# Another order for the first 18 head pairs of cosine attention fused with a hard-swish MLP

## The chip, the cores and the metric

One core of a Trainium2 chip runs the whole program. The metric is the device time of one execution in microseconds (us): the median over several executions. The kernel before takes 426.46 us (median of 4 runs, 425.51 to 426.71).

## The reference

```python
q_n = q / (norm(q, axis=-1) + 1e-6)              # q, k, v: (8, 12, 448, 64)
k_n = k / (norm(k, axis=-1) + 1e-6)
attn = softmax(q_n @ k_n.T / tau)                # tau = 0.1
x = (attn @ v).transpose(0, 2, 1, 3).reshape(3584, 768)
h = x @ w_in                                     # (768, 2048)
g = h * clip(h + 3, 0, 6) / 6
out = g @ w_out                                  # (2048, 768)
```

Since the rows of q_n and k_n have length 1, the scores are bounded, and the kernel leaves the maximum out of the softmax.

## The kernel before, in words

The 8 x 12 heads are worked as 48 pairs (heads n and n + 6 of one batch), six pairs to a batch. Loads go by two pairs: load j brings q or k of pairs 2d and 2d + 1, d = j // 2, and one load of v serves the same two pairs.

For each load there is a chain: LQ (the load, a DMA on SyncE's queue, SP), SQ (squares), RE (sum of each row on VectorE, DVE), NO (four small ACT operations that give one over the norm, for q and k together), NM (multiplication, result in bf16), then a transposition. Loads 0 to 13 are transposed on TensorE (PE) by TR and copied out of PSUM by CQ, CK and CS; loads from 14 on are transposed by a DMA, XD, after which CK (on DVE) and CS (on POOL) only make the padded keys, and scores read the transposed queries in place. VC brings v to bf16. SC multiplies keys by queries, EX takes the exponential on ScalarE (ACT) from PSUM, VA multiplies the result by v and a column of ones into PSUM, FI divides by the sum (a reciprocal and a product on DVE). The attention output of a pair goes transposed into `xT`: by a DMA (XB), or by PE (BK) with a copy (CX).

A batch's six pairs make one `xT`, on which the MLP runs in units. A first-layer unit (kind 1 in ORDER, lines 490 to 521) is 6 matmuls of 448 columns, a relu on ACT (UA) and a product on DVE (UV) into `gT`; a second-layer unit (kind 2, lines 523 to 557) is 16 matmuls of 384 columns, a copy out of PSUM, and two stores on SP. U issues the next unit. W issues the next of eight weight loads on GpSimd's (POOL's) queue, where they are cast to bf16; the first two hold the first half of w_in's columns, the next two the second half, the last four w_out. Units 0 to 7 of a batch need the first two, units 8 to 15 the second two, second-layer units all of w_out.

Nothing schedules this at build time: each engine runs its instructions in the order in which they are written out, and waits where data or a buffer isn't there. For pairs 0 to 17 the order is PLAN, a text of operations; `SQ.5.a.0.7` is the square of load 5 on ACT, columns 0 to 6, and the letter v, p or a names the engine (DVE, POOL, ACT). From pair 18 on a loop (line 682) issues the rest by a fixed pattern. Buffers that tie operations together: 7 for raw loads (LQ j waits for NM j - 7), 3 for raw v, 4 for bf16 v, 2 for squares, 3 for normalised loads, 2 for padded keys, 3 for transposed loads.

PSUM: until OPEN the scores of pairs 0 to 5 alternate between two pairs of banks (SC), while banks Y and Z take transposes. OPEN, after the last exp of pair 5, closes these, and scores, units and transposes then take turns in a ring of six banks (M0, M1, Y, Z, M2, M3): the seventh user waits until the first is read. DP.n and D.n issue n matmuls on zeros whose results are not used, of 248 columns (line 603) and 512 columns (line 598).

Of the kernel before, what the change touches and what calls it, by code (L numbers as in the profile page):

```python
# [15 lines left out]


FIRST = 18
ORDER = "111111111111111111111111111112212222"

PLAN = [
    "DP.4 LQ.1 DP.2 SQ.1.a.11.3 SQ.1.a.0.4 LQ.0 DP.2 LQ.3 SQ.1.a.4.3 DP.5 LQ.2 SQ.0.a.8.6 SQ.0.p.6.2 DP.4",
    "SQ.1.v.7.4 SQ.0.p.0.6 DP.3 RE.1.1 RE.1.0 RE.0.1 DP.1 NO.0.1 LQ.5 DP.4 RE.0.0 SQ.3.a.0.7 DP.2 NO.0.0 NM.1.v.0",
    "NM.0.p.1 DP.8 NM.1.v.1 SQ.2.a.0.7 RE.3 LQ.4 SQ.5.a.0.7 TR.1.Y DP.11 RE.2 NM.0.p.0 SQ.4.p.0.7 CK.0.v TR.0.Z",
    "NO.1 DP.2 CQ.0.v SC.0.0.0 RE.5 DP.3 DP.2 EX.0.0 SC.0.1.1 EX.0.1 DP.3 SC.0.2.0 LV.0 LQ.8 CK.1.v RE.4 LQ.7",
    "EX.0.2 CQ.1.v VC.0.p NM.2.p LQ.6 DP.6 SC.0.3.1 VA.0.0 NM.3.p LV.1 VC.1.v VA.0.1 SC.1.0.0 EX.0.3 VA.0.2 TR.2.Z",
    "VA.0.3 DP.3 SC.1.1.1 LV.2 NO.2 EX.1.0 FI.0 TR.3.Y SC.1.2.0 LQ.9 EX.1.1 NM.4.p CK.2.v VA.1.0 EX.1.2 CQ.2.v",
    "VA.1.1 VC.2.v SC.1.3.1 CQ.3.v NM.5.p SQ.7.p.0.7 SC.2.0.0 DP.2 EX.1.3 VA.1.2 EX.2.0 SC.2.1.1 EX.2.1 CK.3.v",
    "VA.1.3 SC.2.2.0 TR.4.Y BK.0.Z FI.1 SC.2.3.1 DP.2 EX.2.2 DP.1 EX.2.3 CQ.4.v SQ.6.p.0.7 W CX.0.v SC.3.0.0",
    "EX.3.0 CQ.5.v RE.7 TR.5.Z VC.3.v SC.3.1.1 VA.2.0 W VA.2.1 EX.3.1 VA.2.2 VA.2.3 RE.6 CK.4.v SQ.9.a.0.7",  # L30
    "SC.3.2.0 EX.3.2 SC.3.3.1 D.10 LQ.10 LQ.11 SC.4.0.0 CK.5.v FI.2 VA.3.0 NO.3 RE.9 SQ.8.p.0.7 NM.7.p EX.3.3",
    "BK.2.Z RE.8 EX.4.0 SC.4.1.1 VA.3.1 EX.4.1 SC.4.2.0 VA.3.2 EX.4.2 BK.1.Y CX.2.v VA.3.3 SC.4.3.1 LV.3 SC.5.0.0",
    "VC.4.v NM.6.p DP.2 EX.4.3 SC.5.1.1 EX.5.0 TR.7.Z CX.1.v TR.6.Y LV.4 EX.5.1 FI.3 SC.5.2.0 VC.7.p VA.4.0 EX.5.2",
    "VC.6.v CK.6.v NO.4 SC.5.3.1 VA.4.1 EX.5.3 VA.4.2 VC.5.p CS.6.v VA.4.3 DP.5 CQ.6.v CQ.7.v SQ.11.p.0.7 OPEN",
    "SQ.10.p.0.7 CS.7.v CK.7.v FI.4 RE.11 SC.6.0 SC.6.1 EX.6.0 EX.6.1 BK.3 SC.6.2 VA.5.0 NM.8.p VA.5.1 EX.6.2",
    "CX.3.v VA.5.2 VA.5.3 FI.5 SC.6.3 SC.7.0 SC.7.1 TR.8 XB.4 EX.6.3 VA.6.0 LQ.13 VA.6.1 EX.7.0 RE.10 NM.9.p",
    "SC.7.2 EX.7.1 CQ.9.v VA.6.2 EX.7.2 BK.5 TR.9 CQ.8.v LQ.14 CX.5.v SC.7.3 VA.6.3 VC.9.p CK.9.v U NO.5 FI.6 U U",
    "UA UA VA.7.0 EX.7.3 VA.7.1 UA CS.9.v UV W CS.8.v CK.8.v SC.8.0 UV UV SC.8.1 NM.10.p VA.7.2 VA.7.3 FI.7 EX.8.0",
    "SC.8.2 LQ.12 VC.8.p W EX.8.1 TR.10 U LV.5 EX.8.2 UA VA.8.0 CQ.11.v SC.8.3 SQ.13.p.0.7 VA.8.1 CQ.10.v UV",
    "SC.9.0 SC.9.1 EX.8.3 NM.11.p EX.9.0 RE.13 VA.8.2 SC.9.2 VA.8.3 FI.8 EX.9.1 SC.9.3 LQ.15 EX.9.2 U UA TR.11",  # L40
    "SQ.12.p.0.7 EX.9.3 RE.12 CS.11.v VA.9.0 VA.9.1 VC.10.p U CK.10.v XB.6 NO.6 NM.12.p VC.11.p SQ.15.p.0.7",
    "CK.11.v SC.10.0 CS.10.v UV VA.9.2 U UA SC.10.1 EX.10.0 UV UA EX.10.1 SC.10.2 VA.9.3 EX.10.2 LV.6 U UV UA",
    "TR.12 LQ.17 LQ.16 CQ.12.v XB.7 SC.10.3 U SQ.14.p.0.7 NM.13.p UV CQ.13.v SC.11.0 UA RE.15 FI.9 EX.10.3 EX.11.0",
    "U U UV UA UA VA.10.0 SC.11.1 EX.11.1 UV SC.11.2 EX.11.2 VA.10.1 UV VA.10.2 TR.13 SC.11.3 LQ.19 U LV.7 CS.12.a",
    "UA VA.10.3 RE.14 NO.7 SQ.17.p.0.7 NM.15.p CS.13.v CK.13.a U U FI.10 EX.11.3 UA VA.11.0 VA.11.1 VA.11.2",
    "NM.14.p SQ.16.a.0.7 UA CK.12.v SC.12.0 RE.17 XB.8 UV W U VA.11.3 VC.12.p U UV UV EX.12.0 FI.11 SC.12.1 UA",
    "XB.9 UV VC.15.p UA UV EX.12.1 LQ.18 SC.12.2 XB.10 VA.12.0 BK.11 SC.12.3 SC.13.0 EX.12.2 CX.11.v VA.12.1 XD.15",
    "U EX.12.3 EX.13.0 SC.13.1 SC.13.2 UA W U EX.13.1 VA.12.2 RE.16 SQ.19.p.0.7 VC.13.a VA.12.3 EX.13.2 UV SC.13.3",
    "UA U XD.14 FI.12 NO.8 UV SQ.18.p.0.7 CK.14.v U U EX.13.3 U VA.13.0 UA UV SC.14.0 UA UA UA EX.14.0 UV CS.14.v",
    "VC.14.a UV UV SC.14.1 EX.14.1 U SC.14.2 UA NM.16.v RE.19 UV EX.14.2 VA.13.1 U UA U W VA.13.2 UA RE.18 UV UV",  # L50
    "CK.15.v U LQ.20 SC.14.3 UA NO.9 XD.16 UV LQ.21 VA.13.3 U FI.13 U U NM.17.p XD.17 XB.13 UA VA.14.0 UV VA.14.1",
    "SC.15.0 UA EX.14.3 XB.12 VA.14.2 LV.8 UV UA UV EX.15.0 VA.14.3 SC.15.1 W EX.15.1 SC.15.2 FI.14 SQ.21.a.0.7",
    "CK.16.v EX.15.2 SC.15.3 SQ.20.a.0.2 U EX.15.3 U VA.15.0 SQ.20.p.2.5 VA.15.1 NM.19.v RE.20 UV SC.16.0 VC.17.v",
    "CS.16.v SC.16.1 UA CK.17.v SC.16.2 XD.19 EX.16.0 VC.16.v VA.15.2 RE.21 LQ.22 VA.15.3 U EX.16.1 EX.16.2",
    "SC.16.3 FI.15 UA NM.18.p U UV U XD.18 EX.16.3 UA NO.10 VA.16.0 VA.16.1 SC.17.0 SQ.22.p.0.7 SC.17.1 LV.9",
    "VC.18.p UV CK.18.v RE.22 EX.17.0 SC.17.2 VA.16.2 NM.20.v LV.11 XB.14 EX.17.1 VA.16.3 U LQ.23 VC.19.a SC.17.3",
    "UA U EX.17.2 FI.16 XB.16 UV CK.19.v LV.10 CS.18.v EX.17.3 VA.17.0 XB.15",
]


# [1 line left out]
def kernel(  # L62
# [608 lines left out]
    by_kind = {"1": [u for u in stream if u[0] is mm1_unit], "2": [u for u in stream if u[0] is mm2_unit]}  # L671
    first = [by_kind[x].pop(0) for x in ORDER]
    stream = first + [u for u in stream if u not in first]
# [91 lines left out]
```

## Time and profile before

| | |
|---|---|
| median of the runs | 426.46 us |
| the profiled execution | 427.59 us |
| its span, first to last instruction | 425.8 us |
| PE busy | 413.4 us (97%) |
| ACT busy | 271.3 us (64%) |
| DVE busy | 218.3 us (51%) |
| POOL busy | 181.4 us (43%) |
| moved by DMA | 65.82 MB |
| granted TensorE clock, mean | 0.998 |

The numbers below come from one execution taken by the hardware profiler. Matmuls overlap in the records, so the busy time of PE is not its time at full rate: the distance from one matmul's start to the next tells more. A wait in the profile names the instruction or transfer that came last before the waiting instruction could start. The chain of work that ended last is followed back from the last instruction to whatever released each one. SPq and POOLq are instructions that issue DMAs; the time to landing runs from the issue to the completion of the transfer.

### The profile page before, as it was taken

The numbers are of one execution on the slowest core, as the hardware profiler recorded it, in microseconds if no ns is written. First come the engines' busy times: TensorE is split into PE (matmuls) and PEld (weight loads), VectorE is DVE, ScalarE is ACT, GpSimd is POOL, SyncE is SP. The second block draws the span as 40 slices with busy tenths as digits, with TensorE's granted clock in tenths as the row PEclk, the third lists the DMA queues.
The fourth block names the chain that finished last, engine by engine and source line by source line (L and its number), as shares of the span: only waits on it lengthen the run. The fifth ranks groups of instructions, "written<-read, shape, count | busy, mean of one in ns | idle before, by whom it ended". The sixth has DMA issues, their size and how long they took to land.

```text
span 425.8 us, 9251 instructions
## 1 busy us (share of the span) xinstructions
PE 413.4 (97%) x3574; PEld 244.1 (57%) x3575; DVE 218.3 (51%) x419; ACT 271.3 (64%) x593; POOL 181.4 (43%) x184
## 2 busy tenths in 40 slices
PE   7999999899997999999999999999999999999996
PEld 5656655455654555655555555655555555665564
DVE  7689867485425454554555554455554344215410
ACT  6999989787355775676765685576675675105400
POOL 5997787322234474374373473473471310000000
PEclk9999999999999999999999999999999999999999
DMA  8997999997878669767879667567667251330033
GB/s 295 312 232 214 231 180 214 149 205 172 202 186 195 182 157 164 168 167 166 159 190 154 158 155 172 152 168 185 153 156 108 54 81 34 65 78 20 2 75 75
DMA packets 94156, 65.82 MB, mean 155 GB/s; under 512 B 58656, under 2 KB 92576, under 8 KB 94112
## 3 DMA queue, kind: packets, MB, share of 16 engines
q1 hardware_dynamic: 90320, 58.89, 60.6%
q0 software_dynamic: 3712, 6.29, 9.7%
q8 instruction: 28, 0.46, 0.5%
q14 instruction: 16, 0.13, 0.1%
q10 hardware_dynamic: 80, 0.05, 0.0%
HBM read 47.19 MB, written 11.01 MB: 137 GB/s over the span
## 4 chain that ended last, share of the span: by engine, by line
PE 77%; DMA 12%; ACT 4%; DVE 3%; SPq 2%; issue 1%; POOL 1%; ACTq 0%; POOLq 0%; DVEq 0%
PE M L532 21%; PE M L496 18%; PE PV L433 9%; DMA vr<-in_v_dram 5%; PE Y L496 5%; PE Z L532 5%; PE Y L532 5%; PE M L394 5%; PE Z L496 4%; DMA tT<-nrm 3%; ACT at L412 3%; DMA raw<-in_q_dram 2%; PE Z L394 1%; PE SC L394 1%; DVE n L215 1%; DMA xT<-on 1%
## 5 line engine op out<-in xcount | busy, mean ns | idle before, releaser
L532 PEld LDWEIGHTS <-gT 128*128 128x128 bf16 x912 | 88.7, 98 | 58.6
L412 ACT ACTIVATE at<-M 128x448 bf16<-128x448 f32 x195 | 94.8, 565 | 30.1 <-PE M L394 25.3
L496 PEld LDWEIGHTS <-w_in_sb 128*128 128x128 bf16 x768 | 74.2, 98 | 68.7 <-issue 5.0
L532 PE MATMUL M<-w_out_sb,gT 128*128 128x384 bf16 (+1 forms) x640 | 106.0, 322 | 0.0
L496 PE MATMUL M<-xT,w_in_sb 128*128 128x448 bf16 x510 | 104.2, 352 | 0.2 <-DVE gT L511 0.2
L246 POOL TENSOR_TENSOR nrm<-raw,r 128x896 bf16<-128x896 f32 (+1 forms) x45 | 74.3, 1657 | 26.0 <-ACT r L234 22.2
L203 POOL TENSOR_TENSOR sq<-raw 128x896 f32<-128x896 f32 (+3 forms) x42 | 67.8, 1620 | 26.4 <-DMA raw<-in_k_dram 11.4
L511 DVE SCALAR_TENSOR_TENSOR gT<-u,M 128x448 bf16<-128x448 bf16 x85 | 52.4, 620 | 49.8 <-ACT u L505 48.7
L505 ACT ACTIVATE u<-M,half_bias 128x448 bf16<-128x448 f32 x85 | 55.0, 651 | 21.3 <-PE M L496 19.8
L433 PEld LDWEIGHTS <-at 128*128 128x128 bf16 x1344 | 53.3, 98 | 25.5 <-issue 18.3
L433 PE MATMUL PV<-vx,at 128*128 128x65 bf16 (+1 forms) x1344 | 63.9, 198 | 0.0
L215 DVE TENSOR_REDUCE n<-sq 128x14 f32<-128x896 f32 (+1 forms) x50 | 51.9, 1041 | 3.6 <-ACT sq L201 2.4
L351 POOL COPY km<-tT 64x128 bf16<-64x128 bf16 x34 | 10.7, 314 | 99.2 <-DMA tT<-nrm 46.0
L543 ACT COPY o<-M 128x384 f32<-128x384 f32 (+1 forms) x21 | 9.9, 472 | 41.4 <-PE M L532 37.4
L394 PE MATMUL M<-tT,kz 64*128 64x448 bf16 (+1 forms) x172 | 34.3, 353 | 1.5 <-DVE gT L511 0.6
L449 DVE TENSOR_TENSOR on<-PV,rc 128x512 bf16<-128x512 f32 x48 | 33.2, 692 | 3.7 <-DMA xT<-on 2.1
L545 DVE COPY o<-M 128x384 f32<-128x384 f32 (+1 forms) x19 | 10.4, 547 | 47.3 <-PE M L532 44.6
L412 ACT ACTIVATE at<-Y 128x448 bf16<-128x448 f32 x48 | 27.3, 569 | 10.0 <-PE Z L394 10.0
L412 ACT ACTIVATE at<-Z 128x448 bf16<-128x448 f32 x51 | 28.8, 565 | 3.0 <-PE M L394 2.7
L496 PE MATMUL Y<-xT,w_in_sb 128*128 128x448 bf16 x138 | 29.9, 352 | 0.7 <-DMA w_in_sb<-in_moe_w_in_dram 0.7
L448 DVE RECIPROCAL rc<-PV 128x8 f32<-128x8 f32 x48 | 9.9, 206 | 37.7 <-PE PV L433 34.4
L496 PE MATMUL Z<-xT,w_in_sb 128*128 128x448 bf16 x120 | 26.1, 353 | 2.2 <-DMA xT<-on 2.2
(78 smaller groups left out, 345.8 us busy)
## 6 DMA issues: line engine op xcount, KB each, us to landing
vr<-in_v_dram SPq DMA_DIRECT2D x96, 128.0 KB, 3.8
raw<-in_k_dram SPq DMA_DIRECT2D x24, 448.0 KB, 4.3
raw<-in_q_dram SPq DMA_DIRECT2D x24, 448.0 KB, 4.2
out_dram<-o SPq DMA_DIRECT2D x110, 96.0 KB, 2.2
w_in_sb<-in_moe_w_in_dram POOLq DMA_DIRECT2D x4, 768.0 KB, 12.4
w_out_sb<-in_moe_w_out_dram POOLq DMA_DIRECT2D x4, 768.0 KB, 12.9
xT<-on SPq DMA_TRANSPOSE x42, 3.8
tT<-nrm SPq DMA_TRANSPOSE x34, 3.1
```

The source lines that it names most:

```text
L203: engines[e].tensor_tensor(out=o, in0=i, in1=i, op=ALU.mult)
L215: nc.vector.tensor_reduce(out=n2s[d % 2][:, j % 2, c], in_=sq[:, :, :, :].rearrange("p g c d -> p (g c) d")[:, c, :], axis=AX.X, op=ALU.add,)
L246: engines[e].tensor_tensor(out=nrm[:, :, g, :].rearrange("p c g d -> p g c d"), in0=raw_of[j][:, g, :, :], in1=rs[d % 2][3][:, j % 2, :] . ...
L351: nc.gpsimd.tensor_copy(out=km[p, :, p], in_=z[p, 3, :, :])
L394: nc.tensor.matmul(o, ks, qt[rows], start=True, stop=True)
L412: nc.scalar.activation(out=o, in_=x, func=AF.Exp, scale=inv_tau)
L433: nc.tensor.matmul(o, at[:, n, q_cols(i // HP, j)], mv, start=(name == "A0" and j % 2 == 0), stop=last, skip_group_check=True,)
L449: nc.vector.tensor_tensor(out=on[:, :, :, :].rearrange("p (b j) h d -> p b (j h) d", b=2), in0=pv4[:, :, :, 0:D], in1=rc[:, :, :].to_broad ...
L496: nc.tensor.matmul(ps[:, 0:S], w_in_sb[:, cc, fc * 128 : (fc + 1) * 128], x[:, cc, 0:S], start=(cc == 0), stop=(cc == CC - 1),)
L505: nc.scalar.activation(out=u[:, :], in_=ps[:, 0:S], func=AF.Relu, bias=half_bias[:, :], scale=1.0 / 6.0)
L511: nc.vector.scalar_tensor_tensor(out=g[:, fc, c0 : c0 + S], in0=u[:, :], scalar=1.0, in1=ps[:, 0:S], op0=ALU.min, op1=ALU.mult,)
L532: nc.tensor.matmul(ps[:, 0:width], lhs, w_out_sb[:, fc, cols], start=(fc == 0), stop=(fc == FCN - 1),)
```

## The change

The change replaces the text PLAN and the string ORDER; no function is touched. The set of computations stays, but:

- the order of operations is another one throughout PLAN, on all engines and on the DMA queues of SP and POOL;
- ORDER, the kinds of the first 36 units, had `12212222` at its end and now has `11222222` (30 first-layer and 6 second-layer units in both);
- squares of loads 2, 9, 18, 19, 20, 22, 4 and 11 and parts of those of 0 and 1 change engine: 2 and 9 go from ACT to POOL; 4, 11, 18, 19 and 22 from POOL to ACT; 20 is on POOL alone;
- NM: half of load 1 and all of 16 and 20 go from DVE to POOL, 3 and 14 from POOL to DVE;
- VC: 2, 6, 16, 17 from DVE to POOL and 7, 18 from POOL to DVE; 13, 14 and 19 from ACT to POOL; CS.12 and CK.13 from ACT to DVE;
- pairs 1 and 2 go back by DMA (XB) instead of PE and a copy (BK, CX); pairs 4 and 8 the other way;
- DP issues 93 matmuls instead of 77; D.10 moves from pair 3's scores to the very start, ahead of the first transpose;
- the eight W stand earlier, most of all the fifth to eighth.

The whole text is long; these are its lines to about pair 1, the two around OPEN, the stretch around SC.13 and SC.14, and the end:

```diff
-ORDER = "111111111111111111111111111112212222"
+ORDER = "111111111111111111111111111111222222"
...
-    "DP.4 LQ.1 DP.2 SQ.1.a.11.3 SQ.1.a.0.4 LQ.0 DP.2 LQ.3 SQ.1.a.4.3 DP.5 LQ.2 SQ.0.a.8.6 SQ.0.p.6.2 DP.4",
-    "SQ.1.v.7.4 SQ.0.p.0.6 DP.3 RE.1.1 RE.1.0 RE.0.1 DP.1 NO.0.1 LQ.5 DP.4 RE.0.0 SQ.3.a.0.7 DP.2 NO.0.0 NM.1.v.0",
-    "NM.0.p.1 DP.8 NM.1.v.1 SQ.2.a.0.7 RE.3 LQ.4 SQ.5.a.0.7 TR.1.Y DP.11 RE.2 NM.0.p.0 SQ.4.p.0.7 CK.0.v TR.0.Z",
-    "NO.1 DP.2 CQ.0.v SC.0.0.0 RE.5 DP.3 DP.2 EX.0.0 SC.0.1.1 EX.0.1 DP.3 SC.0.2.0 LV.0 LQ.8 CK.1.v RE.4 LQ.7",
...
-    "VC.6.v CK.6.v NO.4 SC.5.3.1 VA.4.1 EX.5.3 VA.4.2 VC.5.p CS.6.v VA.4.3 DP.5 CQ.6.v CQ.7.v SQ.11.p.0.7 OPEN",
-    "SQ.10.p.0.7 CS.7.v CK.7.v FI.4 RE.11 SC.6.0 SC.6.1 EX.6.0 EX.6.1 BK.3 SC.6.2 VA.5.0 NM.8.p VA.5.1 EX.6.2",
...
-    "NM.14.p SQ.16.a.0.7 UA CK.12.v SC.12.0 RE.17 XB.8 UV W U VA.11.3 VC.12.p U UV UV EX.12.0 FI.11 SC.12.1 UA",
-    "XB.9 UV VC.15.p UA UV EX.12.1 LQ.18 SC.12.2 XB.10 VA.12.0 BK.11 SC.12.3 SC.13.0 EX.12.2 CX.11.v VA.12.1 XD.15",
-    "U EX.12.3 EX.13.0 SC.13.1 SC.13.2 UA W U EX.13.1 VA.12.2 RE.16 SQ.19.p.0.7 VC.13.a VA.12.3 EX.13.2 UV SC.13.3",
-    "UA U XD.14 FI.12 NO.8 UV SQ.18.p.0.7 CK.14.v U U EX.13.3 U VA.13.0 UA UV SC.14.0 UA UA UA EX.14.0 UV CS.14.v",
...
-    "SC.16.3 FI.15 UA NM.18.p U UV U XD.18 EX.16.3 UA NO.10 VA.16.0 VA.16.1 SC.17.0 SQ.22.p.0.7 SC.17.1 LV.9",
-    "VC.18.p UV CK.18.v RE.22 EX.17.0 SC.17.2 VA.16.2 NM.20.v LV.11 XB.14 EX.17.1 VA.16.3 U LQ.23 VC.19.a SC.17.3",
-    "UA U EX.17.2 FI.16 XB.16 UV CK.19.v LV.10 CS.18.v EX.17.3 VA.17.0 XB.15",
...
+    "LQ.0 SQ.0.p.0.6 DP.2 DP.4 DP.1 LQ.1 DP.7 DP.2 DP.2 SQ.1.p.7.4 DP.5 SQ.0.v.6.2 DP.2 SQ.0.a.8.6 DP.3 D.10 LQ.2",
+    "DP.3 RE.0.1 SQ.1.a.4.3 RE.0.0 LQ.3 LQ.5 LQ.4 SQ.1.a.0.4 SQ.1.v.11.3 NO.0.0 RE.1.0 SQ.2.p.0.7 RE.1.1 RE.2",
+    "NM.0.p.0 LQ.6 DP.5 NM.0.p.1 LV.0 SQ.3.a.0.7 TR.0.Z NO.0.1 SQ.4.a.0.7 NM.1.p.0 RE.3 NM.1.v.1 DP.4 NO.1 CQ.1.v",
+    "TR.1.Y CQ.0.v VC.0.p CK.0.v DP.5 SC.0.0.0 SQ.5.a.0.7 CK.1.v NM.3.v SC.0.1.1 RE.5 LQ.7 EX.0.0 DP.3 DP.7",
...
+    "SQ.11.a.0.7 CK.7.v VA.4.1 CS.7.v VA.4.2 OPEN VA.4.3 SC.6.0 EX.6.0 W FI.4 NM.9.p VC.6.p SC.6.1 SC.6.2 EX.6.1",
+    "BK.3 VA.5.0 CX.3.v SC.6.3 BK.4 W VA.5.1 EX.6.2 VA.5.2 RE.11 SC.7.0 VA.5.3 SC.7.1 EX.6.3 EX.7.0 CX.4.v FI.5",
...
+    "LQ.17 SC.13.0 EX.13.0 UV VC.13.p SC.13.1 FI.12 U XD.15 SQ.17.p.0.7 XD.14 U UA EX.13.1 UA UV VA.13.0 UV W U UA",
+    "SC.13.2 RE.17 EX.13.2 SC.13.3 UV VC.15.p LQ.20 LQ.18 CK.15.v U EX.13.3 UA CK.14.v VA.13.1 RE.16 U UA W",
+    "SQ.18.a.0.7 NO.8 UV NM.16.p U LV.8 VC.14.p UA U U CS.14.v SC.14.0 UV UA VA.13.2 UA U VA.13.3 UV EX.14.0 UV UV",
...
+    "SC.16.3 VA.15.3 VC.18.v EX.16.2 U SQ.21.a.0.7 EX.16.3 FI.15 NM.19.v VA.16.0 XD.18 VC.19.p XB.15 XD.19 VA.16.1",
+    "UA SC.17.0 VC.17.p EX.17.0 SC.17.1 SC.17.2 LV.10 VA.16.2 LV.11 VA.16.3 U RE.21 U SQ.22.a.0.7 FI.16 EX.17.1 UV",
+    "SC.17.3 EX.17.2 U EX.17.3 CK.18.v XB.16 VA.17.0 CS.18.v UA NO.10 CK.19.v RE.22 NM.20.p UV",
```

## The prediction

> **What bounds the kernel now.** I read the windows first, to find where TensorE (PE) is not fed. PLAN, the only text that changes, covers the first 117.63 us; after it the loop over pairs 18 to 47 runs unchanged code.
>
> ```profile
> 12.14:34.94 22.80, 22.25 (x278) 13.74 (x279) 18.00 (x42) 21.78 (x37) 21.62 (x18) 1.00 1.07 266
> 34.94:53.99 19.05, 18.91 (x240) 11.81 (x240) 16.08 (x38) 17.56 (x43) 12.36 (x11) 1.00 1.04 216
> 53.99:85.00 31.01, 28.48 (x242) 15.06 (x241) 19.38 (x36) 25.76 (x60) 20.84 (x19) 1.00 1.20 182
> 85.00:117.63 32.63, 32.39 (x281) 18.98 (x279) 20.53 (x34) 21.06 (x49) 8.75 (x10) 1.00 0.91 192
> 117.63:140.00 22.37, 19.94 (x180) 11.68 (x178) 8.73 (x17) 13.40 (x32) 9.17 (x9) 1.00 0.82 192
> ```
>
> Columns: length, then busy time of PE, weight load, DVE, ACT, POOL, clock, DMA share. From 12 to 35 us ACT (21.8 of 22.8) and POOL (21.6) are full: the exps of pairs 0 to 5 bound the start, and PE runs dummies between. From 35 us PE is the bound with ACT close behind. The DMA engines are loaded until about 97 us, when the last of the eight weight loads lands. The waits of PE and the chain say which stalls are left:
>
> ```profile
> PE Z L496 <- DMA xT<-on: 2.2, 1, 2.2
> PE Z L394 <- DVE kz L341: 1.0, 1, 1.0
> PE Y L496 <- DMA w_in_sb<-in_moe_w_in_dram: 0.7, 1, 0.7
> ```
> ```profile
> 70.48 12.21 DMA tT<-nrm
> ...
> 128.62 3.91 DMA xT<-on
> ```
>
> PE's timeline puts them at 57.25 us (w_in's fourth load late), 81.89 (the transfer of XD.14, issued at 70.48, lands at 82.69; DVE's key copy CK.14 waits for it and three gT products queue behind), and 130.07 (XB.17 late). Taking start-to-start distances instead of busy times, the steps over full rate are 0.83 us at 57, 0.42 at 72, 2.2 from 81.9 to 84.5, 0.40 at 102, 2.3 at 130 and 0.28 at 138: 6.4 us. The rest of PLAN's lost time is dummies, and some 0.1 us at each change between 64-row score pairs and full-row matmuls.
>
> Why XB.17 is late is in SyncE's (SP's) timeline: its queue is in order, and at the end of PLAN four-piece loads of v (2.66 us of issuing each), stores and transposes stand ahead of it.
>
> ```profile
> 115.10 2.65 SPq L186 DMA_DIRECT2D vr<-in_v_dram  x4
> 117.79 1.28 SPq L480 DMA_TRANSPOSE xT<-on  x1
> 119.11 0.59 SPq L174 DMA_DIRECT2D raw<-in_q_dram  x1
> 119.80 1.46 SPq L553 DMA_DIRECT2D out_dram<-o  x2
> 121.36 1.22 SPq L480 DMA_TRANSPOSE xT<-on  x1
> 122.69 1.17 SPq L553 DMA_DIRECT2D out_dram<-o  x2
> 123.90 2.66 SPq L186 DMA_DIRECT2D vr<-in_v_dram  x4
> 126.61 1.28 SPq L480 DMA_TRANSPOSE xT<-on  x1
> 127.93 0.58 SPq L174 DMA_DIRECT2D raw<-in_k_dram  x1
> 128.62 1.20 SPq L480 DMA_TRANSPOSE xT<-on  x1
> ```
>
> **What the Trainium skill says.** "PSUM — Partial Sum Buffer", Engine vs sequencer instructions: the queues of ScalarE, VectorE and GpSimdE are strict FIFO. The trace agrees: DVE's gT products wait 3.64 us behind CK.14. "DMA: Bandwidth & Descriptors", Queues, rings and completion order: each DMA engine goes round robin between the queues it has work for. Here the weight loads of POOL's queue share with SP's: a 448 KB load takes 3.4 us alone and 14.1 us beside the two w_out loads issued at 70.40 and 72.33. "TensorE: Matmul & The Clock Gate", What's actually happening: the array starts at half clock. The trace agrees: dummies of 248 columns start 0.207 us apart until about 8.0 us and 0.106 after. The page prices 512 columns at 215.7 ns warm; D.10 here shows 216.
>
> **The change part by part.** The same operations are issued, but 93 dummies of 248 columns for 77, some work on other engines, and another order. PE's useful work in PLAN is the same 85.83 us (counted with the trace's spacing: 29 ns a value matmul of 65 columns, 189 ns a score pair, 1.13 us a first-layer unit, 2.60 a second-layer one). So the time is 85.83 plus what PE loses in PLAN plus what the loop loses.
>
> *Start to the first exp.* D.10 and 36 dummies stand before the first transpose: 2.47 + 28 x 0.207 to 8.2, D.10 to 10.4, eight more to 11.2 us. POOL has NM.0 done at about 9.9 (square of load 2 at 6.39 + 1.68, two halves of 0.92), so the dummies delay TR.0 by 1.3 us. TR.1, CQ.0 and CK.0 (0.38 each) put SC.0.0.0 at 13.2. ACT has SQ.4 wait for the sixth load (10.15), then NO.1, SQ.5: 13.1. First exp about 13.6, against 12.14: +1.4.
>
> *First exp to OPEN.* ACT before needs 22.80 us here. SQ.9 (0.9) leaves for POOL. EX.1.0 waits for RE.4 behind NM.3 on DVE until 18.2; from there ACT has 20 two-bank and one-bank exps, NO.3 and NO.4, with no new gap, to about 35.2, against 34.94. POOL, from NM.4 at 18.2, has 11 blocks of 1.68, three VC of 0.61 and two weight issues of 0.75 until VC.6 at about 40: just where VA.6 wants it. Together: +0.3.
>
> *OPEN to EX.10.* Two transposes (BK.1, BK.2) become DMAs before OPEN, where PE had slack, and two (BK.4, BK.8) come back after it: +0.44 us of PE. SQ.11 on ACT: +0.9, on an engine with 1.5 us of idle here. Exps 12.0, two NO 2.1, seven relus 3.7, SQ.11: 18.7 us, so EX.10.0 at 54.4 against 53.99. But units U5 to U7 stand earlier: PE then has about 55.3 us of PLAN left, against 56.3. Net of the three stages: 54.4 + 55.3 - (53.99 + 56.3) = -0.6, taken as -0.5 (bounds -1.5 and +1.0).
>
> *The weight loads.* POOL issues them at about 16, 28, 38, 41, 56, 57, 75 and 76 us instead of 23.06, 23.90, 38.75, 44.45, 70.40, 72.33, 83.33, 85.84. Each takes about 8 to 14 us to land. The fourth lands by 55, U8 needs it at about 57: the 0.83 us stall goes. In return the second has to land by U0 at 41, and SP's loads share with weights for longer.
>
> *The stall at 82.* XD.15 and XD.14 are issued at about 70 and 72, after w_out's first pair rather than beside it, and SC.14.0 comes after 56.99 us of useful work instead of 54.49. Needed at about 85, landing 76 to 80: the 2.6 us at 72 and 82 go. A new wait stands in their place: SQ.18 moves from POOL to ACT. ACT reaches it at about 80.7 and holds NO.8 and U21's relu behind it; load 18, issued at about 74 behind XD.14 and load 20, takes 5 to 14 us. PE first misses U21's bank at U25, about 86.5; after the landing come 0.9 + 1.05 + 0.65 + 0.62 us, so a landing by 83.3 costs nothing and each us later costs one. I expect about 81, and charge 0.9 as the weight of later landings. Net -1.7.
>
> *End of PLAN.* PLAN then ends at about 115. LV.10 and LV.11 stand before U33 instead of around U34 and U35, so XB.17 finds SP's queue empty and is issued when FI.17 is done, about 118; it lands near 122, its unit wants it 12.4 us after PLAN's end, at 127. So 2.3 + 0.28 go, and the 0.40 at 102.
>
> *Sum.* -0.5 - 0.8 - 1.7 - 0.4 - 2.6 = -6.0. Several waits are tight at my accuracy (weight 2 before U0, VC.6, NM.12 before TR.12); I charge 1.5 us for them, from nothing to 5. -4.5 on 426.46: 422.0. The profiled execution is 427.59 with a span of 425.8, 1.1 above the median, so the profile should show a span near 421.3.
>
> **Rivals.** (1) *Only the tail is won:* the new waits in PLAN eat what is won there, and 2.6 us at 130 and 138 remain: 423.9 (423.2 to 425.5). For it: ACT's and POOL's full windows. (2) *Slower through SQ.18:* the price is one us for one after 83.3 us; 88 us (14 us to land, as at 71.76 us before) costs 4.7, 3.8 over my charge; beyond 87.8 with the 1.5 of tight waits at 5 the kernel is slower: 428. For it: DMA transposes beside weight loads; packets of 256 B and of the weights took 2.2 to 3.9 us each around 53 to 56 and 74 to 76 us, a near standstill, and the new order puts XB.1, XB.2, XB.6, XB.7, XB.9 and XB.10 beside weights. Against: load 18 is issued before the seventh weight load carries data. (3) *No change:* the later start is not made up by OPEN (+1.4 instead of +0.3, and PE gets nothing from earlier units), and the tail's gain pays for it and the tight waits: 426.3. (4) *More is won:* no new wait: 420.3.
>
> **How the numbers follow.** Forecast 0.42, rival 1 0.18, rival 2 0.18, rival 3 0.12, rival 4 0.10. A measurement of this kernel tells 0.2% (0.85 us) from no change. The forecast, rivals 1 and 4 are faster, with a few hundredths lost to rival 1's upper end: 0.70 faster; rival 3 gives most of 0.11 same; 0.19 slower. Range: 419.0 (6.0 of gain and 1.4 more of early PE work) to 428.0; the forecast's own is 420.8 to 423.2.
>
> **What would show it.** First exp near 13.6 and the first MATMUL on a ring bank near 35 us; no PE wait over 0.3 us for w_in at U8, for XD.14 at SC.14, or for XB.17 near 127; the loop's first score near 115; XB.17 issued within 1 us of FI.17. Wrong if ACT idles before a square for raw near 81 us, PE waits for w_in near 41, or VA.6 or TR.12 waits on POOL for over 1 us.

## The result, and the profile after

The changed kernel takes 423.77 us (median of 30 runs, 422.51 to 428.86), the kernel before 427.62 us (median of 49 runs beside them, 424.54 to 431.88). The ratio is 0.992 with a 95% interval of 0.9903 to 0.9936: faster by 0.8%. The profiled execution went from 427.59 to 423.95 us, its span from 425.8 to 422.1 us. The forecast was 422.0 us, with a range of 419.0 to 428.0. The ratios, here and below, leave out executions more than 1.5% above the fastest of the same kernel, and so differ a little from the quotient of the medians.

Part of this difference is the granted clock. In the three groups of runs further down, the kernel before has its clock on record for 85 executions: 36 at 0.998 or more (median 426.16 us) and 49 at 0.996 or less (428.52). The changed kernel, here and in two of these groups, has 45 executions at 0.998 or more (423.71) and 5 at 0.996 or less (426.39). So at full clock the change is worth about 2.4 us, and the rest of the 3.85 us is that the clock falls less often. The profile of the kernel before was taken at full clock, but its 427.59 us are more than 29 of those 36 took. What follows compares two single executions; that their difference comes so near to that of the medians is in part luck.

I cut each span at two places that both orders have: OPEN, read as the start of pair 6's first score matmul, and the end of PLAN. The windows of the kernel before (length, then busy time of PE, weight load, DVE, ACT and POOL, clock, DMA share, GB/s), with the middle part also cut at pair 10's first score:

```profile
0.00:34.98 34.98, 31.56 (x342) 20.77 (x344) 27.07 (x74) 29.81 (x57) 29.01 (x39) 1.00 1.01 276
34.98:117.63 82.65, 79.78 (x759) 45.85 (x759) 55.95 (x107) 64.38 (x149) 41.91 (x38) 1.00 1.05 194
34.98:53.21 18.23, 18.14 (x228) 11.32 (x228) 15.39 (x37) 16.87 (x40) 12.32 (x10) 1.00 0.98 220
53.21:117.63 64.42, 61.65 (x532) 34.53 (x532) 40.56 (x71) 47.51 (x110) 29.59 (x28) 1.00 1.07 186
117.63:425.80 308.17, 302.02 (x2477) 177.46 (x2474) 135.24 (x240) 177.12 (x389) 110.53 (x108) 1.00 0.58 130
```

The same windows of the changed kernel:

```profile
0.00:35.61 35.61, 31.40 (x351) 20.79 (x352) 26.32 (x70) 28.70 (x56) 28.99 (x39) 1.00 1.05 266
35.61:116.17 80.56, 79.43 (x767) 46.19 (x767) 56.55 (x113) 66.55 (x147) 39.73 (x41) 1.00 1.02 215
35.61:56.73 21.12, 19.99 (x239) 12.27 (x239) 17.71 (x42) 18.91 (x44) 15.07 (x14) 1.00 1.13 228
56.73:116.17 59.44, 59.44 (x531) 33.92 (x530) 38.84 (x72) 47.64 (x104) 24.66 (x28) 1.00 0.98 210
116.17:422.10 305.93, 301.62 (x2477) 177.25 (x2474) 135.15 (x239) 176.29 (x386) 111.42 (x109) 1.00 0.58 128
```

The start is 0.63 us longer, OPEN to the end of PLAN 2.09 us shorter, the loop, whose code is the same, 2.24 us shorter: 3.7 in all. From pair 10 to the end of PLAN the records leave no gap on PE (59.44 of 59.44). That stretch holds 56.05 us of useful PE work, counted as in the prediction, so 3.39 us are lost in it, where before 64.42 us held 56.97 and lost 7.45. OPEN to pair 10 went the other way: 17.32 us of work in 21.12, where before 15.96 took 18.23.

The waits of PE after, without the first one, of 2.5 us, for the zeros of the dummies:

```profile
PE SC L394 <- ACT at L412: 0.7, 1, 0.7
PE M L496 <- DMA xT<-on: 0.6, 1, 0.6
PE M L291 <- POOL nrm L246: 0.6, 1, 0.6
PE Y L291 <- DVE nrm L246: 0.5, 1, 0.5
PE M L468 <- ACT at L412: 0.4, 1, 0.4
PE M L394 <- ACT at L412: 0.3, 1, 0.3
```

The waits for `w_in_sb` at 57 us, for `kz` behind XD.14 at 82 us and for XB.17 at 130 us, 3.9 us together before, are gone. What is left is small and mostly ahead of pair 10; the wait for `xT` is another one, at 176 us in the loop. In part 4 of the page, the chain that ended last, DMA falls from 12% to 2%, before and after:

```profile
PE 77%; DMA 12%; ACT 4%; DVE 3%; SPq 2%; issue 1%; POOL 1%; ACTq 0%; POOLq 0%; DVEq 0%
```
```profile
PE 90%; ACT 4%; DMA 2%; POOL 1%; DVE 1%; issue 1%; SPq 0%; ACTq 0%; POOLq 0%
```

SP's timeline at the end of PLAN (start, issuing time, line, what is issued) answers to the one of before:

```profile
110.79 5.30 SPq L186 DMA_DIRECT2D vr<-in_v_dram  x8
116.19 2.26 SPq L553 DMA_DIRECT2D out_dram<-o  x2
118.48 1.28 SPq L480 DMA_TRANSPOSE xT<-on  x1
119.86 2.46 SPq L553 DMA_DIRECT2D out_dram<-o  x4
122.36 0.59 SPq L174 DMA_DIRECT2D raw<-in_k_dram  x1
123.06 1.20 SPq L480 DMA_TRANSPOSE xT<-on  x1
```

Both loads of v now stand ahead of the end of PLAN, and XB.17, the last line, is issued at 123.06 instead of 128.62.

Two parts of POOL's timeline after explain what did not go as forecast (the bracket is the idle time before and what ended it):

```profile
6.68 1.68 POOL L203 TENSOR_TENSOR sq<-raw 128x896 f32<-128x896 f32 x1 [0.61 <-ACT nr L232]
8.32 2.73 POOL L246 TENSOR_TENSOR nrm<-raw,r 128x448 bf16<-128x448 f32 x3
...
42.90 1.68 POOL L203 TENSOR_TENSOR sq<-raw 128x896 f32<-128x896 f32 x1 [2.48 <-DVE tT L313]
44.55 3.33 POOL L246 TENSOR_TENSOR nrm<-raw,r 128x896 bf16<-128x896 f32 x2
```

The first is the square of load 2, which landed at 6.52, with NM.0 behind it; the first transpose, TR.0, starts at 10.21, when NM.0's second half is done. The second is SQ.13: load 13 landed at 42.74, 12.5 us after its issue, beside weight loads; NM.11 and NM.10 stood behind it, and TR.10 waited 0.59 us for NM.10.

### The profile page after: what moved, and what is told of

The parts are those of the page before. It is cut to its first block, busy times and chain, and to the rows that moved or that the text cites. A ratio compares the mean times of both kernels' runs of the same rounds, so it can differ in the third digit from the quotient of the medians.

```text
span 422.1 us, 9285 instructions
## 1 busy us (share of the span) xinstructions
PE 412.5 (98%) x3591; PEld 244.2 (58%) x3591; DVE 218.0 (52%) x420; ACT 271.5 (64%) x588; POOL 180.1 (43%) x187
## 4 chain that ended last, share of the span: by engine, by line
PE 90%; ACT 4%; DMA 2%; POOL 1%; DVE 1%; issue 1%; SPq 0%; ACTq 0%; POOLq 0%
PE M L532 23%; PE M L496 22%; PE PV L433 11%; PE Z L496 7%; PE Y L532 6%; PE M L394 6%; PE Y L496 5%; PE Z L532 5%; ACT at L412 3%; PE Z L394 1%; PE PV L603 1%; DMA xT<-on 1%; DMA raw<-in_q_dram 1%; PE SC L394 1%; PE Y L394 1%
## 5 line engine op out<-in xcount | busy, mean ns | idle before, releaser
L412 ACT ACTIVATE at<-M 128x448 bf16<-128x448 f32 x200 | 97.0, 564 | 30.8 <-PE M L394 28.4
L532 PE MATMUL M<-w_out_sb,gT 128*128 128x384 bf16 x592 | 100.8, 326 | 0.0
L246 POOL TENSOR_TENSOR nrm<-raw,r 128x896 bf16<-128x896 f32 (+1 forms) x46 | 75.3, 1641 | 36.8 <-ACT r L234 26.3
L203 POOL TENSOR_TENSOR sq<-raw 128x896 f32<-128x896 f32 (+2 forms) x39 | 63.7, 1634 | 11.3 <-DMA raw<-in_q_dram 6.6
L543 ACT COPY o<-M 128x384 f32<-128x384 f32 x18 | 8.7, 482 | 41.2 <-PE M L532 41.2
L545 DVE COPY o<-M 128x384 f32<-128x384 f32 x19 | 10.6, 558 | 47.0 <-PE M L532 38.0
L394 PE MATMUL M<-tT,kz 64*128 64x448 bf16 (+1 forms) x178 | 33.4, 353 | 0.3 <-ACT at L412 0.3
L532 PE MATMUL Y<-w_out_sb,gT 128*128 128x384 bf16 (+1 forms) x192 | 31.9, 319 | 0.0
L496 PE MATMUL Z<-xT,w_in_sb 128*128 128x448 bf16 x144 | 31.2, 353 | 0.0
L412 ACT ACTIVATE at<-Z 128x448 bf16<-128x448 f32 x47 | 26.5, 564 | 7.1 <-PE M L394 4.1
## 6 DMA issues: line engine op xcount, KB each, us to landing
w_out_sb<-in_moe_w_out_dram POOLq DMA_DIRECT2D x4, 768.0 KB, 10.7
```

What stands on the lines that cost most here:

```text
L203: engines[e].tensor_tensor(out=o, in0=i, in1=i, op=ALU.mult)
L246: engines[e].tensor_tensor(out=nrm[:, :, g, :].rearrange("p c g d -> p g c d"), in0=raw_of[j][:, g, :, :], in1=rs[d % 2][3][:, j % 2, :] . ...
L394: nc.tensor.matmul(o, ks, qt[rows], start=True, stop=True)
L412: nc.scalar.activation(out=o, in_=x, func=AF.Exp, scale=inv_tau)
L496: nc.tensor.matmul(ps[:, 0:S], w_in_sb[:, cc, fc * 128 : (fc + 1) * 128], x[:, cc, 0:S], start=(cc == 0), stop=(cc == CC - 1),)
L532: nc.tensor.matmul(ps[:, 0:width], lhs, w_out_sb[:, fc, cols], start=(fc == 0), stop=(fc == FCN - 1),)
```

## The experiments

Theory A is the prediction's: the new order after about pair 9 removes the three DMA stalls and the late XB.17, and the new first part costs something. Its rivals say that such waits only move, or that what one execution shows is not what the median shows. The runs came in three groups, each beside runs of the kernel before: 427.45 us (median of 45) for the first four, 427.15 (7) for the next four, 427.63 (33) for the last four.

**The changed kernel again.**

> The changed kernel again, beside the other runs of this group. Both theories: 0.992 of the kernel before (interval 0.990 to 0.994), that is 3.4 us less.

423.04 us (422.31 to 423.72), 0.9888 of before (0.9846 to 0.9929); span 421.9. The result repeats, and is a little better than the 0.990 to 0.994 expected; all six executions are at full clock.

**Half of each order.** The operations are taken from one order up to SC.9.0 and from the other for the rest, without the rest's dummies:

```diff
-(old PLAN)
+(old PLAN up to SC.9.0) + (new PLAN, what is not yet done, in its order)     half2_new
+(new PLAN up to SC.9.0) + (old PLAN, what is not yet done, in its order)     half1_new
```

> PLAN of the kernel before up to the first score of pair 9, then what is left to do in the new order. Theory A (the two parts of PLAN act apart: the new order loses 2.6 us up to SC.9 and wins 4.1 from there to the end of PLAN and 2.2 in the loop): 5.5 to 6.3 us less than before, ratio 0.986, span near 420, less than the changed kernel; the wait for the fourth weight load at U8, 0.8 us, may stay. Theory B (the later gain is bought by what the new order does early: weights and v loads issued sooner): no more than the changed kernel's 3.4 us, ratio 0.992 or higher, with waits for DMA at U8, SC.14 or the squares.

> The new order up to the first score of pair 9, then what is left in the old order. Theory A: 2.6 us more than before, ratio 1.006, with the stalls near 82 and 130 us back at 2 us each. Theory B: faster than before or the same (0.995 to 1.000), because the early weights free the DMA queues for the old order too.

The new second half on the old first: 423.4 us (421.59 to 424.88), ratio 0.9906 (0.9868 to 0.9944), profiled span 419.9: the span is Theory A's, the median, 4.0 us less than before, misses its 5.5. The new first half with the old second: 430.8 us (427.18 to 436.61), ratio 1.006 (1.0031 to 1.0089), as Theory A has it. In its profile, of the fastest execution, the late XB.17 is back, and TR.0 waits for POOL (line numbers are one higher in this kernel):

```profile
PE M L497 <- DMA xT<-on: 2.2, 1, 2.2
PE Z L292 <- POOL nrm L247: 1.9, 1, 1.9
```

The stall near 82 us, which Theory A expected too, is not back: XD.14, issued at 73.66 between the fifth and sixth weight load, landed after 7.55 us, and OPEN to the end of PLAN takes 80.19 us instead of 82.65. By the medians, then, the gain comes with the second half, and the first half alone is a loss. In the profile, whose span of 425.4 us is no longer than that of before, the start and XB.17 take back what the middle of PLAN wins, and the stall at 82 is absent with either half in the new order. The clock has a share too: 15 of these 22 executions are at 0.996 or less. For the new second half on the old first, the profile was below the changed kernel's and the timed median was not: the last group takes that up again.

**Only the tail.** The kernel before, with two loads of v and two transposes issued earlier:

```diff
-... SC.17.1 LV.9 ... LV.11 XB.14 ... CK.19.v LV.10 ... VA.17.0 XB.15
+... LQ.21 LV.9 ... LQ.22 LV.10 XB.14 ... XD.18 XB.15
```

> The kernel before with nothing moved but four DMAs of SP's queue: LV.9 and LV.10 up to where LQ.21 and LQ.22 stand, XB.14 behind LV.10 and XB.15 behind XD.18. Theory A (XB.17 was late because SP still had v loads to issue at the end of PLAN): PE's 2.3 us wait for xT at 130 us is gone, 2.0 to 2.6 us less, ratio 0.994 to 0.995. Theory B (the transfer is late for another reason, or the wait moves to the next one, XD.21 at 138 us): within 0.5 us of before, ratio 0.999 to 1.001.

425.29 us (423.46 to 428.3), ratio 0.9967 (0.9945 to 0.9989), span 423.4. The windows of its profile:

```profile
34.97:118.39 83.42, 79.88 (x759) 45.89 (x759) 55.95 (x108) 65.20 (x150) 41.79 (x38) 1.00 1.05 199
118.39:423.40 305.01, 301.34 (x2477) 177.25 (x2474) 135.04 (x240) 176.08 (x386) 110.29 (x108) 1.00 0.58 130
```

The loop falls by 3.2 us, from 308.17 to 305.01, and PLAN is 0.8 us longer (82.65 to 83.42). In the profiles the mechanism is right; four moved tokens are worth 0.33% of the time, 1.4 us, where I had forecast 2.0 to 2.6. At full clock little of that is left: 425.24 us (21 of 22 executions) beside 425.47 (18 of 45). The other 27 of the kernel before are at 0.996 or less, with a median of 428.52, and only one of tail_new is. The stall at 130 us is about as long as the waits after which the clock fell in other profiles (last section), so it may cost more through the clock than by itself. That is not shown, as no execution of the kernel before with a lower clock was profiled.

**The weight loads alone.** W5 and W6, the first two of w_out, are moved up in the kernel before (w56_early), and down in the changed kernel (w56_late), there also with the square of load 18 on POOL instead of ACT (w56_late_sq18p):

```diff
 w56_early
-... XB.8 UV W U ... SC.13.2 UA W U EX.13.1
+... NM.12.p VC.11.p W W SQ.15.p.0.7
 w56_late
-... EX.9.3 W UA UV ... CX.8.v UV W VA.10.0
+... UA NM.15.p W SC.12.0 ... UV VC.13.p W SC.13.1
 w56_late_sq18p, besides
-SQ.18.a.0.7
+SQ.18.p.0.7
```

> The kernel before with only the fifth and sixth weight load moved, from beside XD.15 and XD.14 (70.4 and 72.3 us) up to behind VC.11 on POOL (about 54 us). Theory A (XD.14 lands late because the two w_out loads share the DMA engines with it): XD.14 lands within 7 us, before 78; PE's waits at 72 and 82 us go; 2.0 to 2.6 us less, ratio 0.994 to 0.995. Theory B (the transposes are slow by themselves, or the wait moves to the loads that now share with weights): XD.14 still takes over 9 us, or PE waits elsewhere; within 0.6 us of before.

> The changed kernel with the same two weight loads moved back down, behind NM.15 and VC.13 on POOL (about 69.6 and 71 us), so that XD.15, XD.14 and loads 20 and 18 share with all four w_out loads. Theory A (what the new order wins at 82 us hangs on the early weights): load 18 lands after 85 us instead of 80.5, ACT waits 3 us or more before SQ.18, PE loses 2 to 5 us: ratio to before 0.997 to 1.004. Theory B (SC.14 being 2.5 us of work later is enough): within 0.7 us of the changed kernel, 0.992.

> The run before this one, but with SQ.18 on POOL instead of ACT. Theory A' (the late load hurts through ACT's in-order queue, behind SQ.18): over half of what w56_late lost against the changed kernel comes back. Theory B' (it hurts through XD.14 and CK.14 on DVE, or through w_out landing after U30 wants it): as slow as w56_late, within 0.7 us.

Early in the old order: 433.0 us (430.14 to 435.85), ratio 1.0114 (1.0018 to 1.0209): slower, against Theory A. XD.14 was issued at 76.62 and landed after 5.36 us instead of 12.21, so the stall at 82 went, as A said. But XB.8, XB.9 and XB.10 now met the weights (13.64, 11.85 and 9.97 us to landing), DVE waited, PE stood idle for 2.34 us from 75.45, and the clock was at half from 78.82 to 82.23. The chain (start, length) and DVE's timeline of w56_early:

```profile
63.31 13.64 DMA xT<-on
```
```profile
77.04 0.69 DVE L449 TENSOR_TENSOR on<-PV,rc 128x512 bf16<-128x512 f32 x1 [2.96 <-DMA xT<-on]
```

Late in the new order: 438.82 us (434.24 to 444.46), ratio 1.0209 (1.0115 to 1.0304), far more than Theory A's 1.004. Its profile lost 3.09 and 4.81 us at 37 and 45 us, ahead of the edit, so I read the stages from the variant; why the granted clock is at 0.984 to 0.987 in all four executions is open. That one, 433.28 us (432.4 to 437.48), ratio 1.0135 (1.0055 to 1.0215), has XD.14 issued at 74.33 and landing after 12.84 us, and load 18 after 15.8. The waits of PE, and POOL's timeline, in w56_late_sq18p:

```profile
PE Z L496 <- DVE gT L511: 4.4, 2, 2.9
PE M L394 <- DVE kz L341: 0.5, 1, 0.5
```
```profile
92.68 1.68 POOL L203 TENSOR_TENSOR sq<-raw 128x896 f32<-128x896 f32 x1 [17.22 <-DMA raw<-in_k_dram]
```

With the weight loads back beside XD.14 the stall of before returns in the new order, larger. POOL now waits for load 18 in ACT's place, and 5.5 of some 15 us come back, less than the half that Theory A' wanted and more than Theory B' allows. The clock alone, at 0.988 to 0.996 here and 0.984 to 0.987 there, could account for much of the 5.5 (an estimate: 0.012 of 430 us is 5.2), and the intervals overlap, so neither is decided. Of what is left in the profile, PE's waits of 0.53 and 1.16 us at 87 and 88 us are CK.14's; the longest, 2.92 us from 93.14, is load 18's again: DVE's sum of its squares waits for POOL until 94.39, with a gT product behind it. All executions of these three runs, four of each, are at 0.996 or less, so their times are part stall and part clock. As far as they tell, the place of W5 and W6 matters in both orders, but it is worth something only together with the place of the transposes: the changed order issues them at 56.94 and 57.76, behind XB.6 and XB.7 and 7 us or more ahead of XB.10, XB.9, XD.15 and XD.14.

**The old start, side by side with the changed kernel.** The last group holds the changed kernel as control, the two splices (old order to SC.9 and old order to OPEN, new from there), and the changed kernel without D.10:

```diff
 no_d10
-... SQ.0.a.8.6 DP.3 D.10 LQ.2
+... SQ.0.a.8.6 DP.3 LQ.2
```

> The old order up to OPEN, the new one from there. Theory A (of the 2.6 us that the new order is behind at SC.9, 1.1 come from the start and from two transposes brought behind OPEN, and 1.5 from its order between OPEN and SC.9): 1.1 us less than the changed kernel, span near 421, PE waits between OPEN and SC.9 as in the changed kernel. Theory B (the start is all of it): 2.6 us less, span near 419.5. Theory C (the new order needs its own start): no less than the changed kernel.

> The changed kernel as it is, to stand beside the next three on the same chip. Both theories: 423.0 to 424.2 us, 0.990 to 0.993 of the kernel before.

> The old order up to SC.9, the new one from there, a second time and now beside the changed kernel. Theory A (the new order loses its 2.6 us between OPEN and SC.9, and nothing after depends on it): the old first half is worth 2.6 us, 421.0 us against about 423.6 for the changed kernel, and PE stands at 22.7 us of its PLAN work near 46.5 us instead of 49.2. Theory B (what the old first half wins is lost again in waits that differ from one execution to the next, as the start's wait of TR.0 for POOL did): the same median as the changed kernel within 0.8 us, 422.8 to 424.4.

> The old order up to OPEN, the new one from there, a second time beside the changed kernel. Theory A: OPEN as early as before (35.0 us instead of 35.6), but BK.4, BK.8 and the waits between OPEN and SC.9 stay: 0.6 us below the changed kernel, 423.0. Theory B (the old start has its own wait of TR.0 for POOL's NM, up to 2.4 us in some executions): 423.6 to 425.5, no better than the changed kernel.

> The changed kernel without D.10, the ten dummies of 512 columns (2.2 us) ahead of the first transpose. The prediction's step said that the dummies hold TR.0 back by 1.3 us: then the first exp comes 1.3 us earlier at 11.8 us, and the time is 422.3. Theory A (TR.0 waits for POOL's NM of load 0, and the first exp for ACT's square of load 5, whatever the dummies do): first exp at 12.9 to 13.3 us, PLAN's end and the time unchanged within 0.3 us, 423.3 to 423.9. Rival C (the dummies keep the clock up: without them PE runs at half rate for longer at the start): first exp over 14 us and 424.5 us or more.

| kernel | median, us | range | ratio to before, 95% interval |
|---|---|---|---|
| changed (after_beside) | 425.05 | 423.06 to 429.75, 14 runs | 0.9926 (0.9901 to 0.9951) |
| old to SC.9 (half2_again) | 422.01 | 421.61 to 426.27, 9 runs | 0.9895 (0.986 to 0.9931) |
| old to OPEN (from_open_again) | 421.82 | 421.55 to 423.07, 6 runs | 0.9875 (0.9839 to 0.9911) |
| old to OPEN, earlier (from_open_new) | 422.38 | 421.66 to 424.85, 4 runs | 0.9871 (0.9803 to 0.994) |
| changed, no D.10 (no_d10) | 424.44 | 422.25 to 426.13, 17 runs | 0.9936 (0.9908 to 0.9963) |

The control is slower than the 423.0 to 424.2 us expected. Both splices end below it here, by 3.0 and 3.2 us in the medians, though the intervals of the ratios overlap: from_open_again is the version that I would take over both kernels. How much the old start saves varies, though: in the first group the splice at SC.9 and the changed kernel had stood about equal (423.4 and 423.04 us). Five of the six runs of the old order to OPEN lie below the control's fastest. Theory A's difference for half2_again (2.6 us) is about what came, and for from_open_again (0.6) it was far too small. But A's place for it, the stretch from OPEN to SC.9, is wrong, as the windows of two profiles tell, the control's first and then that of from_open_again:

```profile
0.00:37.96 37.96, 32.87 (x352) 21.61 (x353) 26.44 (x70) 28.50 (x56) 28.96 (x39) 1.00 0.99 255
37.96:117.76 79.80, 79.27 (x768) 46.18 (x767) 56.39 (x113) 66.50 (x147) 39.75 (x41) 1.00 1.00 215
117.76:423.40 305.64, 301.63 (x2477) 177.23 (x2474) 135.09 (x239) 176.09 (x386) 111.16 (x109) 1.00 0.56 128
```
```profile
0.00:35.00 35.00, 30.75 (x343) 20.17 (x344) 27.20 (x74) 29.81 (x57) 28.98 (x39) 1.00 1.00 276
35.00:114.50 79.50, 79.14 (x766) 46.20 (x766) 55.67 (x110) 65.83 (x146) 39.49 (x40) 1.00 0.98 212
114.50:420.20 305.70, 301.64 (x2477) 177.25 (x2474) 135.10 (x239) 176.08 (x386) 111.21 (x109) 1.00 0.57 128
```

After OPEN both do the same matmuls, BK.4 and BK.8 included, and differ by 0.30 us. The 2.96 us before OPEN are the difference, and most of that is one load. The profiles in one table, in us, with the landing of the third load issued (load 2 in the new order, load 3 in the old):

| kernel | third load lands | TR.0 | OPEN | OPEN to end of PLAN | loop |
|---|---|---|---|---|---|
| before | 6.39 | 10.69 | 34.98 | 82.65 | 308.17 |
| tail_new | 6.61 | 10.68 | 34.97 | 83.42 | 305.01 |
| half2_new | 6.76 | 10.70 | 34.99 | 79.63 | 305.27 |
| half2_again | 6.46 | 10.68 | 34.98 | 79.62 | 305.30 |
| from_open_again | 6.45 | 10.71 | 35.00 | 79.50 | 305.70 |
| from_open_new | 8.60 | 12.47 | 38.24 | 79.50 | 305.36 |
| changed, first profile | 6.52 | 10.21 | 35.61 | 80.56 | 305.93 |
| after_again | 7.12 | 10.81 | 36.20 | 79.79 | 305.91 |
| after_beside | 8.65 | 12.34 | 37.96 | 79.80 | 305.64 |
| no_d10 | 7.42 | 11.11 | 36.52 | 79.79 | 305.19 |
| half1_new | 8.45 | 12.13 | 37.84 | 80.19 | 307.37 |

In the five rows with the new start TR.0 comes 3.68 or 3.69 us after the third load, with D.10 and without: SQ.2 on POOL takes 1.68 and the two halves of NM.0 0.92 each. OPEN follows TR.0 by 25.4 to 25.7 us. With the old start TR.0 comes at 10.7 as long as the load lands by about 6.8 (10.69 less the 3.87 of the row with 8.60), so it has 0.3 us in hand, and OPEN is 0.6 us earlier than in the best profile of the new start. When the load is 2 us late the old start is no better: TR.0 at 12.47, OPEN at 38.24. Not all of that is the load: PE stood idle for 2.22 us until TR.0, the clock was at half from 14.14 to 17.55, and OPEN came 25.77 us after TR.0 instead of 24.3. So 0.6 us of the splices' advantage is a property of the order, as far as these profiles tell. The rest of the difference between these two profiles is that one execution had a late load and the other had none; that the medians of this group differ by 3 us for the same reason is likely, not shown, since how often a load is late in either order I did not measure. The clock is not the reason: all six executions of from_open_again and 13 of the control's 14 are at 0.998 or more. The fastest runs allow 0.6 or more: 421.55 to 421.66 for the splices, 422.31 to 423.06 for the changed kernel in its several groups.

The run without D.10 does not settle the dummies. Its first exp came at 14.02 us, not at Theory A's 12.9 to 13.3, since its third load landed at 7.42; its median is near the control's (424.44 beside 425.05, ratios with overlapping intervals), but near Rival C's 424.5 as well. PE's timeline of no_d10 at the start:

```profile
7.62 1.69 PE L603 MATMUL PV<-xT 128*128 128x248 bf16 x11
11.11 0.56 PE L291 MATMUL Z<-ident,nrm 128*128 128x128 bf16 x7 [1.81 <-POOL nrm L246]
```

In this execution 1.81 of D.10's 2.2 us turn into waiting for NM.0, and the clock holds: SC.0.0.0 starts 2.50 us after TR.0 with D.10 (12.71 in the first profile) and 2.51 without (13.62). The medians hide more. Without D.10, 10 of 17 executions are at 0.996 or less (median 425.35 us) and 7 at full clock (422.53); with it, 1 of 14 and 13 (424.91). So dropping D.10 may save time where the clock holds, and Rival C's colder clock cost it where it does not. A third load a microsecond later than this one would stretch the wait of 1.81 us past the 2.2 us after which the clock fell elsewhere. That this is what happens is not shown: no execution of no_d10 with the lower clock was profiled.

## Why the prediction was right, and which steps were not

The time, 423.77 us, is inside the range, 1.8 us above the forecast and just outside the forecast's own 420.8 to 423.2; the span is 422.1 where 421.3 was forecast. The sum of its terms was -4.5 us after a charge of 1.5; the profiles have -3.7 and the medians -3.85, from a median of before that was itself 1.2 us above the 426.46 of the forecast. The prediction read one profile and had no term for a clock that falls in some executions and not in others, which makes about a third of the gain in the medians; that the sum of the stalls comes near the measured gain is partly luck.

**Start to the first exp.** Forecast 13.6, measured 13.12. The step that failed in this execution is "the dummies delay TR.0 by 1.3 us". The clock warmed up at 5.55 us, not at 8.03 as in the profile of before (the spacing of the dummies falls from 207 to 106 ns there), the last dummy started at 9.83, and TR.0 waited for NM.0. The prediction had both terms of that, "POOL has NM.0 done at about 9.9", and the wrong one came out as the later. It need not always: in the control the clock warmed up at 8.21 and the last dummy started at 11.13, so with a third load at 6.52 instead of 8.65 the dummies would have held TR.0 back by about 1 us (an estimate from 6.52 + 3.69). "TensorE: Matmul & The Clock Gate", What's actually happening, in the Trainium skill says the array starts at half clock; a moment of warming up taken from one profile can't be carried to another (5.6 to 8.4 us in the fourteen profiles).

**OPEN.** Forecast 35.2, measured 35.61, and 36.2 to 38.0 in the four other profiles of this start in the table. The prediction had the tie, NM.0 behind the square of the third load on POOL, but took 6.39 us for that load's landing and had no term for a later one.

**OPEN to EX.10.** The failed step is the net of -0.5 for the three stages up to EX.10. "PE then has about 55.3 us of PLAN left, against 56.3" was right within a us (56.05 against 56.97), but EX.10.0 came at 57.12, not 54.4. Against the old order, pair 10's scores are 3.52 us later with 0.92 us more done: 2.6 us lost. Of these 0.63 are OPEN's (a wait of 0.44 us for ACT ends there), 0.44 the work of BK.4 and BK.8, and 1.5 are lost after OPEN: by start distances 0.59 us at 36 us for ACT, which has SQ.11 and pair 5's last exp ahead of pair 6's, 0.76 at 47 for NM.10, and small steps. I had put SQ.11 on ACT's idle time; it stood on the path at OPEN. The wait at 47 is in one of four profiles of the changed order (80.56 against 79.79 to 79.80 in the table). The charge of 1.5 for tight waits covered this in size; the wait that came, NM.10 before TR.10, is a neighbour of the one I had named, NM.12 before TR.12.

**The weight loads.** Issued at 16.21, 26.80, 36.83, 39.73, 56.94, 57.76, 76.87 and 78.23 us, all within 2.3 us of the forecast; the second is later than before (23.90), the others earlier. The fourth landed at 54.94, U8 ran at 59.62 without a wait: right.

**The stall at 82.** XD.15 and XD.14 were issued at 69.72 and 71.77 and took 6.2 and 4.9 us; SC.14.0 started at 85.77 (forecast about 85) without a wait. Load 18 was issued at 75.09 and landed at 80.46 (about 81). SQ.18 ran at 83.01 on ACT without waiting for it, so the charge of 0.9 was not needed. w56_late and its variant show what this rests on: with the fifth and sixth weight load some 13 us later (69.51 and 70.89 in the variant), the same order takes 9 to 15 us more, part of it through the clock. "DMA: Bandwidth & Descriptors", Queues, rings and completion order, has the engines go round robin between queues; it is in line with that that the two weight loads of the kernel before took 14.62 and 16.74 us and load 18 of the other queue, between them, 14.11.

**End of PLAN.** PLAN ended at 116.17 (about 115). XB.17 was issued at 123.06, not 118: FI.17's product was done at 118.84, but XB.16, four stores and a load stood ahead of it on SP. It landed at 126.83, still in time, so 2.3 and 0.28 us were won as forecast. 0.79 us came back at 176.31, where an XB issued at 172.41 took 4.84 us: a net of 2.24 for 2.6.

**The rivals.** Rival 1's time, 423.9, is the nearest to the median, but its cause isn't what happened: in the profiles the middle of PLAN did win (2.09 us, 2.85 in three other profiles), and the tail gave 2.2, not everything. Rival 2's price for a late load 18 showed only where the weights were moved. Rival 3's later OPEN is real (+0.63), but the stretch after pair 10 more than made it up: 4.06 us less lost, where the three terms of -0.8, -1.7 and -0.4 add up to 2.9.

## What to carry to other kernels

Of two orders with the same work, compare the stretches between events that both have, and count work done at each, so that time and work moved across a boundary don't pass for a gain. An instruction in a strict queue that waits for a load makes everything behind it depend on that load: here a square moved ahead of the first normalisation on POOL tied the start of the whole kernel to the third load. Before medians are compared, the executions are best divided by their granted clock: here that separates what the order saves at full clock from how often the clock falls. Transfers that get into each other's way are best moved as a group: the weight loads moved alone took the stall to the next transposes (w56_early).

## What the runs showed of the hardware

**One slow part of a load.** The third load's lateness is that of one or two of its parts. "DMA: Bandwidth & Descriptors", Why a DMA increments its semaphore by 16 and not by 1, says that up to 16 DMA engines finish independently, and only the full 16 means that all data has landed. The trace has the 16 completion events of load 2 one by one (us):

```
changed, first profile   6.03 6.09 6.10 6.11 6.13 6.16 6.18 6.20 6.22 6.24 6.28 6.29 6.40 6.41 6.46 6.52
after_beside             6.10 6.18 6.22 6.24 6.25 6.26 6.28 6.29 6.30 6.32 6.34 6.35 6.37 6.38 7.27 8.65
half1_new                6.06 6.08 6.13 6.16 6.20 6.23 6.24 6.26 6.29 6.30 6.32 6.33 6.34 6.40 6.43 8.45
```

Fifteen of sixteen land within 0.4 us (in half1_new; fourteen within 0.3 us in the control), and the last one 2 us later. The first two loads are not late (4.10 and 5.21 in the control), and the following ones keep the lag of the third (9.77, 10.90). Why one part falls behind in some executions is open.

**Transposes beside weights.** A DMA transpose of `nrm` or `on` lands 2.4 to 5 us after its issue in the quieter stretches, and after 7 to 16 us where it meets weight loads on POOL's queue: XD.14 12.21 (before), 12.84 (w56_late_sq18p) and 7.55 (half1_new), XB.8 13.64 (w56_early), an XB issued at 42.51 in the kernel before 16.15. The loads of k issued right behind are caught as well: 14.11 us before, 14.9 and 15.8 in w56_late_sq18p. It is not a matter of overlap alone: in the changed kernel XB.10 was issued at 64.64, with the weight loads of 56.94 and 57.76 landing at 67.40 and 71.72, and took 7.39 us. What sets the size I did not take apart.

**The clock after a wait of PE.** Once the clock had warmed up, six waits of PE in the fourteen profiles left it idle for 2.22 us or more in one piece: 2.22 us (from_open_new, from 10.25), 2.34 (w56_early), 2.92 (w56_late_sq18p), 3.09, 4.81 and 6.48 (w56_late). With each, the granted clock was at half for 3.41 us (6.83 for the longest), beginning between 1.4 us before the wait's end and 1.7 us after it, and at no other time between warm-up and the last microseconds. Waits of 2.17 us and less had no such stretch: 2.15 at 130 us (before), 2.17 there (half1_new), 2.12 at 135 (w56_early). PE work at half rate for 3.41 us comes to 1.7 us lost (an estimate), and one stretch takes 0.4% from the mean clock of some 425 us: 0.996 instead of 1.000.
